# Convolution and routed expert network in one kernel: where a step's copies, the weights' stores and the first rows stand in the order

## Chip, cores and metric

The kernel runs on 1 core of one Trainium2 chip. The metric is the device time of one execution in microseconds (us). Three runs of the kernel before took 964.08, 965.21 and 965.73; the median is 965.21.

## What is computed

```python
def _attn_ref(x, weight_gen):
    w = np.exp(weight_gen - np.max(weight_gen, axis=-1, keepdims=True))
    w = w / (np.sum(w, axis=-1, keepdims=True) + 1e-09)
...
    out = np.einsum('bshk,bskhg->bshg', w, x_unf)

def _moe_ref(x, w_skip, w_gate, w1, w2):
    do_compute = x @ w_skip > 0
    out = x.copy()
    xc = x[do_compute]
    logits = xc @ w_gate
    e_idx = np.argmax(logits, axis=1)
...
    for e in range(E):
        mask = e_idx == e
        h = np.maximum(xc[mask] @ w1[e], 0.0)
        y[mask] = gate_w[mask, None] * (h @ w2[e])
    out[do_compute] = xc + y
```

A causal convolution over 7 positions, with weights that are a softmax per token and head, runs over 8 sequences of 3584 tokens with 192 features. Its output rows go into a mixture of 8 experts with 1024 hidden features: a row with a positive skip score is sent to the expert of its highest gate logit, and the expert's answer, times the gate's softmax, is added to the row. The other rows pass unchanged.

## The kernel before, in words

**Convolution.** The tokens are cut into 16 chunks of 4 steps, 64 steps in all. What a step issues, and in which order, stands in a string of tokens in `SEQ`, one of four by the step's place in its chunk; the engines execute what they are given in that order. The tokens that matter here: `x` loads the step's input (L276); `a`, `b` build band matrices on DVE (L323); `C`, `G` are the convolution's matmuls (L342), `c`, `e` copy their result to SBUF on ACT (L349). `K` (`back`) transposes that result on TensorE (L358) and forms the logits (L361), into three PSUM tiles. `O` (`back_out`) copies these out on ACT: acc twice (L372) and ls (L374). `L`, `l`, `H`, `R`, `r`, `W` turn a chunk's logits into each row's expert and place in the expert's bucket in DRAM, and queue the chunk's 16 scatters. `P` takes one piece of the preparation of the experts' weights. `F` takes one piece of the expert network's flow, sends one scatter on POOL (L483) and advances the clock `tick` by one. `M` assigns a pair (256 rows of one expert), `D` (`ahead`) fetches assigned pairs.

**Weights.** For each expert in turn (`prep_expert`, L201) two raw halves are loaded (L198), ACT takes absolute values with a running sum (L207) whose output goes into the expert's own weight tile, small matmuls and DVE find scales (L213 to L227), POOL clears the tile's last columns (L228), and ACT and DVE split the weights into f16 high and low parts (L229, L235 to L243). Six DMAs on SP store the tile to `wsp` in DRAM (L246 to L249). These tiles have the tag `wst` with 4 buffers, and a pair's fetch takes its tile from the same 4. A fetch (L611) reads the pair's rows from the buckets (L619) and its weights from `wsp` in three DMAs (L631) at a place that a register gives.

**Expert network.** `flow` (L746) takes pairs in turn. `prep_rows` (L634) gives a row scale: absolute sums on ACT (L641), DVE (L644 to L647), the high part on ACT (L650), the low part on DVE (L653, L656), then eight transposes on TensorE (L663), copied by ACT (L664). A pair has four up steps: ten matmuls (L676), the ReLU's f16 high part hh on ACT (L680), the low part hl on DVE (L686), and two steps later twelve down matmuls (L696). The result is added to the rows (L702) and scattered to the output (L707). There are 57 pairs. The first flow starts `LEAD` ticks after its fetch. PSUM has 3 buffers with tag `s` (the three of `K`, the transposes, and others), 3 for the ups and the convolution, 2 for the downs. After the last step only pairs are left, from about 776 us on; this is called the tail.

An F token that falls between K and O is taken only in part:

```python
    def advance(held=False):
        if held and (turning[0] or not ffn[0]):
            return
```

Of the kernel before, what the change touches and what calls it, by code (L numbers as in the profile page):

```python
# [11 lines left out]
F16 = mybir.dt.float16  # L12
F32 = mybir.dt.float32
I32 = mybir.dt.int32
AF = mybir.ActivationFunctionType
# [36 lines left out]
SEQ = [  # L52
# [4 lines left out]
]  # L57
# [4 lines left out]
XG = 6  # L62
LEAD = 5
BEHIND = 2
DEAL = 5
# [10 lines left out]
def conv_moe_kernel(ctx, tc, x, wg, w_skip, w_gate, w, out):  # L76
# [29 lines left out]
    def pop():  # L106
        if outs:
            outs.pop(0)()
        elif unsent:
            send(*unsent.pop(0))  # L110
    wsp = dram.tile([E, P, WC], F16, name="wsp")
    img = [dram.tile([K, P, R_], F32, name=f"img{i}") for i in range(2)]
# [60 lines left out]
    for t in img:  # L173
        nc.sync.dma_start(t.rearrange("m p r -> (m p r)").rearrange("(p c) -> p c", p=P), zero[:, 0:K * R_])

    dummy = cst.tile([P, RW], F32, name="dummy")
    nc.vector.memset(dummy, 0.0)
# [9 lines left out]
    heads = cst.tile([1, 2, E], F32, name="heads")  # L187
    nc.vector.tensor_copy(heads[:, 0, :], iof[:, 0:E])
    nc.vector.tensor_scalar(heads[:, 1, :], ecap[0:1, :], -float(TRASH), None, op0=ALU.add)
# [3 lines left out]
    most = cst.tile([1, E + 1], F32, name="most")  # L193
    nc.vector.memset(most[:, E:E + 1], E * TT * float(P) - 0.5)

    def load_part(e, i):
# [4 lines left out]
    def prep_expert(e, raws):  # L201

        a, b, c = raws[0][:, 0:FF], raws[0][:, FF:], raws[1]
        m = st.tile([P, 2], F32, tag="wm", name="wm")
        wo = sl.tile([P, WC], F16, tag="wst", name="wst", bufs=4)
        for i in range(2):
            nc.scalar.activation(wo[:, 0:3 * FF // 2], raws[i], AF.Abs, accum_out=m[:, i:i + 1])  # L207
            yield
# [10 lines left out]
        nc.tensor.matmul(pm[:, 2 * P:2 * P + 2], ones2, dg, start=True, stop=True)  # L219
        yield  # L220
        mv = st.tile([P, 2], F32, tag="wmv", name="wmv")
        nc.vector.tensor_scalar(mv, pm[:, 2 * P:2 * P + 2], 1e-30, None, op0=ALU.max)
# [20 lines left out]
        nc.vector.scalar_tensor_tensor(wo2[:, :, D:2 * D], c3, s2, wo2[:, :, 0:D], op0=ALU.mult, op1=ALU.subtract)  # L243
        yield
        for i in range(2):
            nc.sync.dma_start(wsp[e, 0:64, 2 * FF + i * FF // 2:2 * FF + (i + 1) * FF // 2], bh[64 * i:64 * (i + 1), :])  # L246
            nc.sync.dma_start(wsp[e, 64:P, 2 * FF + i * FF // 2:2 * FF + (i + 1) * FF // 2], bl[64 * i:64 * (i + 1), :])
        nc.sync.dma_start(wsp[e, :, 0:2 * FF], wo[:, 0:2 * FF])
        nc.sync.dma_start(wsp[e, :, 3 * FF:], wo[:, 3 * FF:])  # L249

# [267 lines left out]
    def assign(T, F, final):  # L518
# [42 lines left out]
        yield  # L561
        nc.vector.tensor_scalar(so[:, :, 0], ef, float(E - 1), None, op0=ALU.min)
        yield
# [5 lines left out]
        yield  # L569
        todo.extend((so, i, T, None) for i in range(F))  # L570
        told.extend([tick[0] + BEHIND] * F)

    def assign_one(T):
# [25 lines left out]
        yield  # L599
        todo.append((so, 0, T, counted[0]))  # L600
        told.append(tick[0] + BEHIND)

# [7 lines left out]

    def fetch(so, i, T, upto):  # L611

        NT = P * T
        er = nc.values_load(so[0:1, i, 0:1], engines=[ET.SP], min_val=0, max_val=E - 1,
                            skip_runtime_bounds_check_because="clamped to the experts on the chip")
# [14 lines left out]
        for c0, c1 in ((0, 2 * FF), (2 * FF, 4 * FF), (4 * FF, WC)):  # L630
            nc.sync.dma_start(wt[:, c0:c1], wsp[ds(er, 1), :, c0:c1].rearrange("a p c -> p (a c)"))  # L631
        return T, wt, xg
# [50 lines left out]
    def up_low(ph, hh):  # L683

        hl = sl.tile([P, 512], F16, tag="hl", name="hl", bufs=3)
        nc.vector.scalar_tensor_tensor(hl, ph, 0.0, hh, op0=ALU.max, op1=ALU.subtract)  # L686
        return hh, hl
# [46 lines left out]
    def pairs():  # L734

        while True:
            if auto[0]:
                ahead(3)
            if not ready:
                return  # L740
            if ready[0][3] + LEAD > tick[0] and not auto[0]:
                return
            T, wt, xg, _ = ready.pop(0)
            yield wt, xg, 0

    def flow():  # L746
# [25 lines left out]
        while cur:  # L772
            py = ps_y.tile([P, 2, 256], F32, tag="py", name="py")
            new = None
            for f2 in range(NFB // 2):
# [8 lines left out]
                while len(done_) > (f2 < 1):  # L784
                    finish(*done_.pop(0))
                late.append((cur, py, f2, up_low(*h)))
                if f2 == 0 and len(rows) < 2:
                    new = begin()
                    if new:
                        rows.append(new)  # L790
                        next(new[1])
                if new and f2 == 1:
                    next(new[1])
                if rows and f2 == 2:
# [11 lines left out]
    def advance(held=False):  # L806
        if held and (turning[0] or not ffn[0]):
            return
        if ffn[0] is None and ready and ready[0][3] + LEAD <= tick[0] and START <= step[0]:
            ffn[0] = flow()  # L810
        elif ffn[0] and next(ffn[0], ffn) is ffn:
            ffn[0] = None
# [196 lines left out]
```

## Time and profile before

| | us |
|---|---|
| median of 3 runs | 965.21 |
| lowest and highest | 964.08, 965.73 |
| profiled execution | 956.43 |
| its span in the profile | 954.5 |
| TensorE busy (PE) | 814.2 (85%) |
| VectorE (DVE) | 659.5 (69%) |
| ScalarE (ACT) | 474.3 (50%) |
| GpSimd (POOL) | 403.9 (42%) |

The span is the profiled stretch of one execution. TensorE's granted clock is 0.927 of full speed on the mean. Busy shares are averages over three very different parts: preparation and convolution to some 160 us, all three kinds of work to 250 us, convolution and experts to 771 us, and the tail. Waits are listed by the engine that waits and the work that ended the wait; SPq is SP's DMA queue, and times are from the span's start.

### The profile page before, as it was taken

Reading aid. Unit: us, or ns where it says so; the run is one execution under the profiler, and the core shown is the slowest. Engines: PE = TensorE matmul, PEld = TensorE weight load, DVE = VectorE, ACT = ScalarE, POOL = GpSimd, SP = SyncE. Lnnn points to the kernel's source line nnn. Section 1 sums busy time; section 2 is a strip of 40 time slices with the busy share of each in tenths; the row PEclk is TensorE's granted clock in tenths of the full one; section 3 lists DMA queues with packets and bytes.
Section 4 is the critical chain, followed back from the end, with each engine's and each line's share of the span. In section 5 each row is a group of like instructions: output and inputs, shape, how many; then the busy total and the mean of one; then the engine's idle time right before and its main releaser. Section 6 shows DMA issues by size and latency. Waiting matters only on the chain. (4 is left out here: it accounts for less than half of the span.)

```text
span 954.5 us, 36775 instructions
## 1 busy us (share of the span) xinstructions
PE 814.2 (85%) x15248; PEld 694.1 (73%) x15248; DVE 659.5 (69%) x1945; ACT 474.3 (50%) x1141; POOL 403.9 (42%) x415
## 2 busy tenths in 40 slices
PE   0567853778799997999899998999999899999997
PEld 0446633567587886888788786887888789899996
DVE  4888974746877785878686876687675566855553
ACT  0456655454555544555445463555555455455552
POOL 1008883243344536354626372545454353712122
PEclk9787775877799997999999999999999999999999
DMA  6588698897687569576868595768576559876540
GB/s 225 179 291 280 223 305 300 303 323 237 193 283 269 187 229 307 169 246 229 261 190 274 174 299 166 245 201 263 189 267 201 164 196 287 272 257 219 194 158 19
DMA packets 99176, 221.33 MB, mean 232 GB/s; under 512 B 16144, under 2 KB 54859, under 8 KB 97216
## 3 DMA queue, kind: packets, MB, share of 16 engines
q1 hardware_dynamic: 81248, 197.22, 62.2%
q0 software_dynamic: 17760, 21.75, 7.2%
q8 instruction: 120, 1.97, 0.8%
q14 instruction: 48, 0.39, 0.1%
HBM read 152.97 MB, written 77.80 MB: 242 GB/s over the span
## 5 line engine op out<-in xcount | busy, mean ns | idle before, releaser
L483 POOL DMA_INDIRECT bucket<-acc,ixi x256 | 279.2, 1091 | 320.9 <-DVE wst L229 68.0
L676 PE MATMUL ph<-xT,wst 128*128 128x256 f16 x2280 | 296.7, 279 | 20.2 <-DVE hl L686 12.8
L676 PEld LDWEIGHTS <-wst 128*128 128x128 f16 x2280 | 219.8, 100 | 59.5 <-issue 22.4
L680 ACT ACTIVATE hh<-ph 128x512 f16<-128x512 f32 x228 | 135.8, 595 | 243.3 <-PE ph L676 239.9
L686 DVE SCALAR_TENSOR_TENSOR hl<-ph,hh 128x512 f16<-128x512 f32 x228 | 155.8, 684 | 144.6 <-ACT hh L680 144.4
L696 PE MATMUL py<-wst,hh 128*128 128x192 f16 x1824 | 247.0, 248 | 0.0
L696 PE MATMUL py<-wst,hl 128*128 128x192 f16 x912 | 225.6, 247 | 2.8 <-issue 1.9
L707 POOL DMA_INDIRECT out_dram<-xg x114 | 117.1, 1027 | 225.5 <-DVE xg L702 171.7
L342 PE MATMUL bt<-bd,xt 64*32 64x56 f32 x8192 | 125.7, 232 | 59.3 <-DVE bd L323 27.9
L696 PEld LDWEIGHTS <-hh 128*128 128x128 f16 x1824 | 164.3, 99 | 15.8 <-issue 9.4
L342 PEld LDWEIGHTS bt<-bd,xt 64*32 64x32 f32 x8192 | 100.9, 113 | 92.2 <-issue 47.3
L323 DVE TENSOR_TENSOR bd<-rot,mask 128x896 f32<-128x896 f32 x128 | 137.0, 1080 | 8.8 <-DMA rot<-img 8.8
L696 PEld LDWEIGHTS <-hl 128*128 128x128 f16 x912 | 89.8, 98 | 3.4 <-issue 2.1
L664 ACT COPY xT<-pt 128x512 f16<-128x512 f16 x114 | 61.4, 590 | 57.2 <-PE pt L663 57.2
L702 DVE SCALAR_TENSOR_TENSOR xg<-py,fc,xg 128x192 f32<-128x192 f32 x114 | 42.2, 411 | 64.7 <-PE py L696 60.6
L349 ACT COPY xs<-bt 128x448 f32<-128x448 f32 x128 | 66.0, 539 | 37.0 <-PE bt L342 36.8
L358 PE MATMUL pa<-ident,xs 128*112 128x128 f32 x512 | 77.8, 298 | 1.6 <-ACT xT L664 1.1
L650 ACT ACTIVATE xs<-xg,rs 128x192 f16<-128x192 f32 x114 | 45.7, 449 | 44.1 <-DVE rs L647 31.0
L358 PEld LDWEIGHTS pa<-ident,xs 128*112 128x112 f32 x512 | 63.1, 147 | 5.1 <-ACT xT L664 2.8
L663 PE MATMUL pt<-ident,xs 128*128 128x128 f16 x456 | 41.7, 226 | 24.0 <-ACT acc L372 13.2
L372 ACT COPY acc<-pa 112x384 f32<-112x384 f32 x128 | 55.0, 481 | 1.6 <-PE pa L358 1.5
L663 PEld LDWEIGHTS <-xs 128*128 128x128 f16 x456 | 30.1, 100 | 31.1 <-DVE xs L656 19.7
(152 smaller groups left out, 734.3 us busy)
## 6 DMA issues: line engine op xcount, KB each, us to landing
wst<-wsp SPq DMA_DIRECT2D x114, 512.0 KB
wst<-wsp SPq DMA_DIRECT2D x57, 520.0 KB
xt<-in_x_dram SPq DMA_DIRECT2D x64, 384.0 KB
out_dram<-acc SPq DMA_DIRECT2D x16, 1358.0 KB
raw<-in_moe_w_dram SPq DMA_DIRECT2D x16, 768.0 KB
xg<-bucket SPq DMA_DIRECT2D x57, 194.0 KB
rot<-img SPq DMA_DIRECT2D x16, 448.0 KB
wt<-in_weight_gen_dram SPq DMA_DIRECT2D x16, 392.0 KB
```

The costliest lines, as they stand in the source:

```text
L323: nc.vector.tensor_tensor(bd.rearrange("p h (m u) -> p h m u", m=K), rot_[c][:, :, i0 * H:(i0 + 2) * H].rearrange("p m h -> p h m").unsque ...
L342: mm = nc.tensor.matmul(bt[a][GP * j:GP * (j + 1), c0:c0 + QH], xt[p0:p1, b0:b0 + GP], bd_[k, i // 2][p0:p1, i % 2 * H + h, :], start=True ...
L349: nc.scalar.copy(xs_[k][:, 2 * a:2 * a + 2, :], bt_[k][a][:, 0:2 * QB * QH].rearrange("p (x c) -> p x c", x=2))
L358: nc.tensor.transpose(pa[j][0:Q, x * P:(x + 1) * P], xs[:, x, j * Q:(j + 1) * Q], ident)
L483: i = nc.gpsimd.indirect_dma_start(out=bviews[t], out_offset=bass.IndirectOffsetOnAxis(ap=rt_[c][:, t:t + 1], axis=0), in_=acc_[c][:, t, : ...
L663: nc.tensor.transpose(pt[:, 2 * i2 + i, :], xs[:, t, i2, i * P:(i + 1) * P], ident16)
L664: nc.scalar.copy(xT[:, :, t * P:(t + 1) * P], pt)
L676: mm = nc.tensor.matmul(ph[:, fi * 2 * P:(fi + 1) * 2 * P], wt[:, a * FF + f0:a * FF + f0 + P], xT[:, cc, :], start=j == 0, stop=j == 4)
L680: nc.scalar.activation(hh, ph, AF.Relu)
L686: nc.vector.scalar_tensor_tensor(hl, ph, 0.0, hh, op0=ALU.max, op1=ALU.subtract)
L696: mm = nc.tensor.matmul(py[:, t, 0:D], l[:, a], w2v[:, f, r, :], start=f == 0 and t == 0 and j == 0, stop=f == NFB - 1 and j == 2, skip_gr ...
L707: i = nc.gpsimd.indirect_dma_start(out=oviews[nsc[0] % 8], out_offset=bass.IndirectOffsetOnAxis(ap=xg[:, t0 + t, D + 1:D + 2].bitcast(I32) ...
```

## The change

Five things change. (1) `wsp` becomes a two-dimensional tensor, and each expert's stores go through a view of its own; a fetch is given by hand the stores of the experts prepared when its pair was assigned. Expert numbers that lead to a fetch are scaled by 128, and one small store writes 30 columns of `wsp` at the start. (2) The absolute values go to a fixed scratch `spare`, and the expert's weight tile is taken five pieces later, after the scale matmuls. (3) `O` stands right behind `K` in each step. (4) In up step 1 the low parts of the next pair's rows (L653, L656) are issued ahead of hl (L686). (5) The first pair is told 4 ticks after its assignment instead of 2, and its flow starts 7 ticks after its fetch instead of 5.

```diff
@@ -50,18 +50,17 @@
 SEQ = [
-    "O x F C a D F G w P L F l D c b T M P F e 2 P F H P F D P T M K F P",
-    "O x F C R a D F G W r R P F W r R D c b T M P F W r e 3 P F P F W D P T M K F P",
-    "O x F C W r R a D P F G W r V P F W D 5 c b T M P F e P F P F D P T M K F P",
-    "O x F C a D P F G 4 P F D c b T M P F e 0 P F P F D 1 P T M K F P",
+    "x F C a D F G w P L F l D c b T M P F e 2 P F H P F D P T M K O F P",
+    "x F C R a D F G W r R P F W r R D c b T M P F W r e 3 P F P F W D P T M K O F P",
+    "x F C W r R a D P F G W r V P F W D 5 c b T M P F e P F P F D P T M K O F P",
+    "x F C a D P F G 4 P F D c b T M P F e 0 P F P F D 1 P T M K O F P",
 ]
...
-LEAD = 5
-BEHIND = 2
+LEAD, BEHIND = (5, 7), (2, 4)
@@ -108,7 +107,9 @@
-    wsp = dram.tile([E, P, WC], F16, name="wsp")
+    wsp = dram.tile([E * P, WC], F16, name="wsp")
+    wviews = dram_disjoint_views(wsp[:, :], E)
+    stored = []
@@ -173,6 +174,7 @@
+    nc.sync.dma_start(wsp[0:1, 6 * FF + 2:WC], zero[0:1, 0:15].bitcast(F16))
@@ -185,7 +187,7 @@
-    nc.vector.tensor_copy(heads[:, 0, :], iof[:, 0:E])
+    nc.vector.tensor_scalar(heads[:, 0, :], iof[:, 0:E], float(P), None, op0=ALU.mult)
@@ -193,6 +195,8 @@
+    spare = cst.tile([P, 3 * FF // 2], F16, name="spare")
@@ -202,9 +206,8 @@
-        wo = sl.tile([P, WC], F16, tag="wst", name="wst", bufs=4)
         for i in range(2):
-            nc.scalar.activation(wo[:, 0:3 * FF // 2], raws[i], AF.Abs, accum_out=m[:, i:i + 1])
+            nc.scalar.activation(spare, raws[i], AF.Abs, accum_out=m[:, i:i + 1])
@@ -218,6 +221,7 @@
         nc.tensor.matmul(pm[:, 2 * P:2 * P + 2], ones2, dg, start=True, stop=True)
         yield
+        wo = sl.tile([P, WC], F16, tag="wst", name="wst", bufs=4)
@@ -242,11 +246,14 @@
+        to = wviews[e][e * P:(e + 1) * P, :]
+        stored.append([])
         for i in range(2):
-            nc.sync.dma_start(wsp[e, 0:64, 2 * FF + i * FF // 2:2 * FF + (i + 1) * FF // 2], bh[64 * i:64 * (i + 1), :])
...
+            stored[e].append(nc.sync.dma_start(to[0:64, half], bh[64 * i:64 * (i + 1), :]).ins)
...
+        stored[e].append(nc.sync.dma_start(to[:, 0:2 * FF], wo[:, 0:2 * FF]).ins)
+        stored[e].append(nc.sync.dma_start(to[:, 3 * FF:], wo[:, 3 * FF:]).ins)
@@ -597,8 +604,8 @@
-        todo.append((so, 0, T, counted[0]))
-        told.append(tick[0] + BEHIND)
+        todo.append((so, 0, T, counted[0], n))
+        told.append(tick[0] + BEHIND[given[0] == 1])
@@ -628,7 +635,10 @@
         for c0, c1 in ((0, 2 * FF), (2 * FF, 4 * FF), (4 * FF, WC)):
-            nc.sync.dma_start(wt[:, c0:c1], wsp[ds(er, 1), :, c0:c1].rearrange("a p c -> p (a c)"))
+            i = nc.sync.dma_start(wt[:, c0:c1], wsp[ds(er, P), c0:c1])
+            if paced[0]:
+                for j in chain(*stored[:most_e]):
+                    after(i, j, "the weights of an expert")
@@ -783,14 +793,14 @@
+                if new and f2 == 1:
+                    next(new[1])
                 late.append((cur, py, f2, up_low(*h)))
                 if f2 == 0 and len(rows) < 2:
                     new = begin()
                     if new:
                         rows.append(new)
                         next(new[1])
-                if new and f2 == 1:
-                    next(new[1])
@@ -806,7 +816,7 @@
-        if ffn[0] is None and ready and ready[0][3] + LEAD <= tick[0] and START <= step[0]:
+        if ffn[0] is None and ready and ready[0][3] + LEAD[spent[0] == 0] <= tick[0] and START <= step[0]:
```

**ACT, around the first pair's rows.** xs,S are its sums (L641, L651 in the change), raw the weights of e5. Before:

```order
L641 ACTIVATE xs,S_2525<-xg 128x192 x2
L389 COPY L<-lt 112x4x2x9 x2
L349 COPY xs_2536<-bt 128x448
L650 ACTIVATE xs<-xg,rs 128x192 x2
L349 COPY xs_2536<-bt 128x448
L207 ACTIVATE wst,wm<-raw 128x1536 x2
L372 COPY acc<-pa 112x2x192 x2
L374 COPY ls<-pl 128x224
L664 COPY xT<-pt 128x4x128 x2
L427 ACTIVATE dl<-dl 112x128
L680 ACTIVATE hh<-ph 128x512
```

With the change:

```order
L356 COPY xs_2530<-bt 128x448 x2
L210 ACTIVATE spare,wm<-raw 128x1536 x2
L379 COPY acc<-pa 112x2x192 x2
L381 COPY ls<-pl 128x224
L651 ACTIVATE xs,S_2606<-xg 128x192 x2
L434 ACTIVATE dl<-dl 112x128
L660 ACTIVATE xs<-xg,rs 128x192 x2
L449 COPY qf<-rk 128x136
L356 COPY xs_2722<-bt 128x448 x2
L674 COPY xT<-pt 128x4x128 x2
L239 ACTIVATE wst<-raw,wsc 128x1024
L690 ACTIVATE hh<-ph 128x512
```

The sums stood at the head of this piece, in front of the L copies; now the L copies stand above the piece and the sums behind the absolute values and the step's acc and ls copies. The first split of e5 (L239) now stands ahead of the first hh.

**SP and DVE, the stores of e4 and the first write into e5's tile**, with the semaphores waited for (DMAHW lanes are used by SP's DMAs in turn). SP before, then with the change:

```order
L246 DMA wsp<-wst 64x512 [waits DMAHW3_49,DMAHW4_49,DMAHW1_49,DMAHW7_49,DMAHW0_49,Activation_49]
L247 DMA wsp<-wst 64x512 [waits DVE_49]
L246 DMA wsp<-wst 64x512 [waits DMAHW5_49]
L247 DMA wsp<-wst 64x512 [waits DMAHW6_49]
L248 DMA wsp<-wst 128x2048
L249 DMA wsp<-wst 128x3104 [waits DVE_49,Activation_49,Pool_49]
```

```order
L253 DMA wsp<-wst 64x512 [waits DMAHW2_49,DMAHW4_49,DMAHW1_49,DMAHW5_49,DMAHW0_49,Activation_49]
L254 DMA wsp<-wst 64x512 [waits DVE_49]
L253 DMA wsp<-wst 64x512 [waits DMAHW6_49]
L254 DMA wsp<-wst 64x512 [waits DMAHW7_49]
L255 DMA wsp<-wst 128x2048
L256 DMA wsp<-wst 128x3104 [waits DVE_49,Pool_49]
```

DVE before, then with the change, around the write of e5's scale into its tile (L229, L233):

```order
L227 TENSOR_TENSOR wsc<-wsc,wsf 128x2 [waits DVE_49]
L229 TENSOR_SCALAR wst<-wmv 128x1 [waits DMAHW3_49,DMAHW2_49,DMAHW7_49,DMAHW0_49,Pool_49]
L580 SCALAR_TENSOR_TENSOR most<-most,pick 1x8
L584 TENSOR_REDUCE bm<-most 1x1 [waits DVE_49]
L587 TENSOR_SCALAR bo<-most,bm 1x8 [waits DVE_49]
L590 TENSOR_TENSOR bb<-heads,bo 1x16 [waits DVE_49]
L592 SCALAR_TENSOR_TENSOR heads<-bo,heads 1x8 [waits DVE_49]
L238 SCALAR_TENSOR_TENSOR wst<-raw,wsc,wst 128x1024 [waits DMAHW5_49,Activation_49]
```

```order
L231 TENSOR_TENSOR wsc<-wsc,wsf 128x2 [waits DVE_49]
L233 TENSOR_SCALAR wst<-wmv 128x1 [waits DMAHW5_49,DMAHW4_49,DMAHW6_49,DMAHW1_49,DMAHW7_49,DMAHW0_49,Pool_49]
L587 SCALAR_TENSOR_TENSOR most<-most,pick 1x8
L591 TENSOR_REDUCE bm<-most 1x1 [waits DVE_49]
L594 TENSOR_SCALAR bo<-most,bm 1x8 [waits DVE_49]
L597 TENSOR_TENSOR bb<-heads,bo 1x16 [waits DVE_49]
L599 SCALAR_TENSOR_TENSOR heads<-bo,heads 1x8 [waits DVE_49]
L242 SCALAR_TENSOR_TENSOR wst<-raw,wsc,wst 128x1024 [waits Activation_49]
L696 SCALAR_TENSOR_TENSOR hl<-ph,hh 128x512 [waits Activation_49]
```

The first store waits for five lanes in both, moved by one. DVE's write waited for four lanes and POOL and now waits for six lanes and POOL; hl stands behind it. The six lanes 4, 5, 6, 7, 0, 1 are those that e4's six stores have in turn.

**DVE, up step 1 of a pair in the tail** (S is the next pair's row sums). Before:

```order
L644 TENSOR_SCALAR S_17973<-S_17973 128x2
L645 TENSOR_SCALAR S_17973<-S_17973 128x2
L647 RECIPROCAL rs<-S_17973 128x2
L702 SCALAR_TENSOR_TENSOR xg<-py,fc,xg 128x192 x2
L686 SCALAR_TENSOR_TENSOR hl<-ph,hh 128x512
L653 SCALAR_TENSOR_TENSOR xs<-xg,rs,xs 128x192 x2
L656 COPY xs<-xs 128x2x64 x2
L686 SCALAR_TENSOR_TENSOR hl<-ph,hh 128x512
L666 SCALAR_TENSOR_TENSOR fc<-S_17973,wst,xg 128x2
```

With the change:

```order
L654 TENSOR_SCALAR S_17975<-S_17975 128x2
L655 TENSOR_SCALAR S_17975<-S_17975 128x2
L657 RECIPROCAL rs<-S_17975 128x2
L712 SCALAR_TENSOR_TENSOR xg<-py,fc,xg 128x192 x2
L663 SCALAR_TENSOR_TENSOR xs<-xg,rs,xs 128x192 x2
L666 COPY xs<-xs 128x2x64 x2
L696 SCALAR_TENSOR_TENSOR hl<-ph,hh 128x512 x2
L676 SCALAR_TENSOR_TENSOR fc<-S_17975,wst,xg 128x2
```

L653 and L656 moved ahead of the hl that stood in front of them.

## Rows read from the trace of the kernel before

**Rows 1.** Windows view: stretch, length; busy of PE, PEld, DVE, ACT, POOL; clock, DMA share, GB/s.
```profile
140.00:160.00 20.00, 10.20 (x173) 7.64 (x173) 8.13 (x21) 8.00 (x18) 9.79 (x13) 0.50 0.83 275
...
180.00:200.00 20.00, 14.38 (x235) 11.40 (x233) 9.34 (x20) 10.68 (x20) 8.14 (x8) 0.86 0.97 349
776.00:940.00 164.00, 159.41 (x1721) 147.43 (x1720) 99.43 (x335) 85.61 (x213) 52.45 (x55) 1.00 0.65 216
```

**Rows 2.** ACT's timeline from 157 to 203 us (start, duration, instruction, idle before and releaser).
```profile
157.05 0.36 ACT L641 ACTIVATE xs<-xg 128x192 f16<-128x192 f32 x1 [9.65 <-DMA xg<-bucket]
...
163.49 0.36 ACT L374 COPY ls<-pl 128x224 f32<-128x224 f32 x1
...
170.87 0.60 ACT L680 ACTIVATE hh<-ph 128x512 f16<-128x512 f32 x1 [3.57 <-PE ph L676]
...
179.53 1.15 ACT L235 ACTIVATE wst<-raw,wsc 128x1024 f16<-128x1024 f32 x1 [4.80 <-DVE wsc L227]
...
181.67 1.56 ACT L240 ACTIVATE wst<-raw,wsc 128x1536 f16<-128x1536 f32 x1
...
183.87 0.36 ACT L374 COPY ls<-pl 128x224 f32<-128x224 f32 x1
...
195.69 1.48 ACT L207 ACTIVATE wst<-raw 128x1536 f16<-128x1536 f32 x1 [6.26 <-PE py L696]
...
202.94 0.36 ACT L374 COPY ls<-pl 128x224 f32<-128x224 f32 x1
```

**Rows 3.** SP's timeline, the issues of weights and their stores, 154 to 180 us.
```profile
154.45 0.41 SPq L619 DMA_DIRECT2D xg<-bucket  x1
...
170.21 0.51 SPq L246 DMA_DIRECT2D wsp<-wst  x1
...
173.36 0.37 SPq L249 DMA_DIRECT2D wsp<-wst  x1
...
179.38 2.21 SPq L631 DMA_DIRECT2D wst<-wsp  x3
```

**Rows 4.** SP's waits over the program (total us, times, longest).
```profile
SPq L246 <- DMA wst<-wsp: 28.2, 6, 8.2
```

**Rows 5.** ACT's timeline in the tail, the hh at equal places of two pairs.
```profile
809.63 0.60 ACT L680 ACTIVATE hh<-ph 128x512 f16<-128x512 f32 x1 [1.49 <-PE ph L676]
...
818.87 0.60 ACT L680 ACTIVATE hh<-ph 128x512 f16<-128x512 f32 x1 [1.49 <-PE ph L676]
```

**Rows 6.** TensorE's waits over the whole program.
```profile
PE pt L663 <- ACT acc L372: 13.2, 4, 4.2
```

**Rows 7.** TensorE's waits from 300 to 771 us.
```profile
PE ph L676 <- DVE hl L686: 8.0, 12, 1.6
PE pt L663 <- ACT acc L372: 6.1, 2, 3.6
```

**Rows 8.** DVE's timeline at one pair of the tail.
```profile
813.48 0.68 DVE L686 SCALAR_TENSOR_TENSOR hl<-ph,hh 128x512 f16<-128x512 f32 x1
814.08 0.74 DVE L653 SCALAR_TENSOR_TENSOR xs<-xg,rs,xs 128x192 f16<-128x192 f32 x2
814.85 0.29 DVE L656 COPY xs<-xs 128x128 f16<-128x128 f16 x2
```

**Rows 9.** TensorE's timeline: the rows' transposes and next up, with and without a wait.
```profile
814.58 0.22 PE L663 MATMUL pt<-ident,xs 128*128 128x128 f16 x1
...
815.50 1.26 PE L676 MATMUL ph<-xT,wst 128*128 128x256 f16 x10
...
258.06 0.61 PE L663 MATMUL pt<-ident,xs 128*128 128x128 f16 x8
258.51 1.25 PE L676 MATMUL ph<-xT,wst 128*128 128x256 f16 x10
```

**Rows 10.** TensorE's waits in the tail, 776 to 940 us.
```profile
PE pt L663 <- DVE xs L656: 3.3, 17, 0.3
```

**Rows 11.** TensorE's timeline, the program's first up.
```profile
168.89 1.94 PE L676 MATMUL ph<-xT,wst 128*128 128x256 f16 x10
```

More of the change, by code (lines that the diff above doesn't have):

```diff
@@ L244, in prep_expert @@
         yield
+        to = wviews[e][e * P:(e + 1) * P, :]
+        stored.append([])
         for i in range(2):
-            nc.sync.dma_start(wsp[e, 0:64, 2 * FF + i * FF // 2:2 * FF + (i + 1) * FF // 2], bh[64 * i:64 * (i + 1), :])
-            nc.sync.dma_start(wsp[e, 64:P, 2 * FF + i * FF // 2:2 * FF + (i + 1) * FF // 2], bl[64 * i:64 * (i + 1), :])
-        nc.sync.dma_start(wsp[e, :, 0:2 * FF], wo[:, 0:2 * FF])
-        nc.sync.dma_start(wsp[e, :, 3 * FF:], wo[:, 3 * FF:])
+            half = slice(2 * FF + i * FF // 2, 2 * FF + (i + 1) * FF // 2)
+            stored[e].append(nc.sync.dma_start(to[0:64, half], bh[64 * i:64 * (i + 1), :]).ins)
+            stored[e].append(nc.sync.dma_start(to[64:P, half], bl[64 * i:64 * (i + 1), :]).ins)
+        stored[e].append(nc.sync.dma_start(to[:, 0:2 * FF], wo[:, 0:2 * FF]).ins)
+        stored[e].append(nc.sync.dma_start(to[:, 3 * FF:], wo[:, 3 * FF:]).ins)
     prepared, open_, prepares = [0], [0], [0]
@@ L561, in assign @@
         yield
-        nc.vector.tensor_scalar(so[:, :, 0], ef, float(E - 1), None, op0=ALU.min)
+        nc.vector.tensor_scalar(so[:, :, 0], ef, float(E - 1), float(P), op0=ALU.min, op1=ALU.mult)
         yield
@@ L569, in assign @@
         yield
-        todo.extend((so, i, T, None) for i in range(F))
-        told.extend([tick[0] + BEHIND] * F)
+        todo.extend((so, i, T, None, E) for i in range(F))
+        told.extend([tick[0] + BEHIND[0]] * F)
     def assign_one(T):
@@ L609, in together, with fetch @@
                     gs.remove(g)
-    def fetch(so, i, T, upto):
+    def fetch(so, i, T, upto, most_e):
         NT = P * T
-        er = nc.values_load(so[0:1, i, 0:1], engines=[ET.SP], min_val=0, max_val=E - 1,
+        er = nc.values_load(so[0:1, i, 0:1], engines=[ET.SP], min_val=0, max_val=(E - 1) * P,
                             skip_runtime_bounds_check_because="clamped to the experts on the chip")
@@ L740, in pairs @@
                 return
-            if ready[0][3] + LEAD > tick[0] and not auto[0]:
+            if ready[0][3] + LEAD[0] > tick[0] and not auto[0]:
                 return
```

## The prediction

> **What bounds the kernel now.** I read the stretches first [rows 1]. From 776 us on only the expert network (FFN) is left: TensorE is busy 159.41 of 164 us, at full clock. So little can be won per pair there, but what is won counts in full, since nothing else sets the end. Between 140 and 200 us the picture is the opposite: TensorE is busy 10.2 of the first 20 us and 14.4 of the last 20, the granted clock is 0.50 and 0.86 there, and the DMA share 0.83 and 0.97. That is the stage in which the convolution runs, the experts' weights are still prepared, and the first pairs start.
>
> What stops that stage is seen on ACT [rows 2], whose copies of the logits (ls, L374) mark the end of each step. Step 16 ends at 163.49, step 17 at 183.87 and step 18 at 202.94, so the last two take 20.4 and 19.1 us. Two stalls stand inside. **Stall A**: ACT waits 9.65 us, until 157.05, for the rows of the first pair; everything in ACT's queue waits with it. **Stall B**: ACT waits 6.26 us, until 195.69, to write absolute values of e6's weights into a weight tile whose last user is pair 0's final down matmul. Between them ACT starts e5's split at 179.53 after 4.80 us.
>
> SP shows why the rows come late and what follows [rows 3]: the fetch of pair 0 goes out at 154.45, and after pair 1's SP stands until 170.21 in front of e4's weight stores. That wait is for the pairs' own weight loads [rows 4], 28.2 us in 6 times, 8.2 the longest. The last of e4's stores is issued at 173.36; pair 2's weights, which must not be read before these stores, go at 179.38 and SP shows no wait for them, so they have landed by then.
>
> **The change, part by part.**
>
> *Views of the weights in DRAM, the extra small store, scaled heads.* The order shows that the first store of e4 still waits for five DMA lanes, the same set as before moved by one, because one DMA more was issued ahead. I therefore count on the wait of [rows 4] staying: 0 us. If the views did remove it, e4's stores could leave 8.2 us earlier, at 162; that is a rival below. The extra store is one DMA issue on SP, about 0.4 us by the 0.41 of [rows 3], in the opening stage where SP is ahead: 0, at most 0.4.
>
> *Absolute values to a scratch, first rows later.* These two act on the same stage and are counted together. The order on ACT shows the first pair's L641 behind the step's Abs and its acc and ls copies instead of ahead of the L copies. What was queued behind the 9.65 us is no longer behind it, so step 16 can end some 8 us sooner. But the weight tile of e5 is now taken five pieces later, after pairs 0, 1 and 2 have taken theirs, so it falls to the tile that e4 was stored from. ACT's first split of e5, DVE's scale (L229 before) and POOL's memset must then wait for all six of e4's stores. Those leave only at 170.21 to 173.36, for a reason that the change does not touch. They land after 173.36+0.37 and by 179.38; I take 178, near the later end, because the DMA stays loaded and raw weights are queued behind. Behind that wait stand on ACT the first hh, step 17's copies, and on DVE the first hl and the next band; TensorE and the scatters follow them.
>
> So step 17 is not freed. From the start of e5's split, ACT needed 183.87-179.53=4.34 us to reach ls. In the new order the third split (1.56 us at 181.67) comes behind the copies, leaving about 2.8 to 3.3: 178+3.2=181.2, a gain of about 2.7 us at step 17. In exchange the first hh, at 170.87 before, is behind the same wait, and by the order 1 instead of 3 up groups have been issued at that point. Stall B then goes entirely, since Abs needs no weight tile: 6.3 us, of which I count 5, since e6's own first write now waits for e5's stores, which are late next. Together steps 17 and 18 come about 8 us earlier, with 2 up groups owed. A full up step (10 ups and 12 downs) costs a quarter of a pair; the hh of 809.63 and 818.87 are four apart, so 9.24/4=2.3 us [rows 5], and the debt is 4.6 us, repaid in a stage where TensorE is the bound. Net 8-4.6=3.4. The transposes that waited for the acc copies in this stage (L663 behind L372: 13.2 us in 4 over the whole program, of which 6.1 in 2 after 300 us [rows 6, 7], so 7.1 in 2 here) give about a third more, 2.6, the rest lying inside stalls already counted. **Early stage: -6.** Bounds: all of A, B and the 4.80 gone without a debt would be 20.7; I take -16 as the far end since the DMA share is 0.97 from 180 to 200 and bytes do not shrink. The other end is +6: no gain, and 2 up groups plus some clock.
>
> *A step's copies right behind its transposes.* After 300 us this takes away pt<-acc, 6.1 us in 2 [rows 7]; some of it returns, because hh and the preparation's pieces now stand behind the copies. *Rows' parts ahead of low parts* shows in the steady stage the other way round: hl now follows 1.03 us of L653 and L656, and ph<-hl is already 8.0 us in 12 there [rows 7]. I take **-2** for both, between -6 and +3.
>
> *Rows' parts ahead of low parts, in the tail.* Here the price can be read [rows 8, 9]. On DVE the hl of 813.48 stands ahead of L653 (814.08) and L656 (814.85, two copies to 815.14). TensorE starts the first transpose at 814.58 and the next up at 815.50, 0.92 later, with a wait for L656 in between. Where nothing waited, at 258.06, the next up (258.51) follows 0.45 after the first transpose. With hl behind, the rows' parts end about 0.6 earlier, at 814.5, in time. So at most 0.47 us a pair is won; the wait is shown 17 times, 17x0.47=8.0 in all. The idle alone is 3.3 us in those 17 [rows 10], the lower end. I take 0.36 a pair, nearer the upper end, because the idle counts empty time alone, while the distance from start to start is what the next up sees: 17x0.36=6, **-6**, from -3 to -8. What covers the hl that now ends near 815.2: its down matmuls come behind the whole next up (1.26 us from 815.50), so not before 816.7. If that cover were gone, the 0.6 would come back on TensorE.
>
> **Sum.** -6-2-6=-14. The profiled execution took 956.43 us (its span is 954.5 and 1.9 lie around it); 956.43-14=942.4. The median of the runs shown is 965.21, 8.8 above the profiled one, so the forecast is **951 us**.
>
> **The clock, read against a rule.** At 168.89 the ten matmuls of an up took 1.94 us, at 815.50 1.26 [rows 9, 11]; the granted clock of 0.50 from 140 to 160 is the lower of its two levels (1.2 of 2.4 GHz), and it is 0.86 from 180 to 200 [rows 1]. The first ups now come about 8 us later. If the clock then stayed at the lower level through 180 to 200, the 14.38 us of TensorE work there would be 14.38x0.86/0.50=24.7, which is 10.3 more: 951+10=961. The Trainium skill ("TensorE: Matmul & The Clock Gate", section "Part 1: The HAM clock gate") says that the throttled state is the default and that activity releases it; by that rule a later start of the FFN speaks for this case. The rows agree in direction. But the convolution's matmuls go on in that stretch and will be denser, so I give it 0.06.
>
> **Rivals.**
> 1. *The stall only moves* (0.20). e5's split waits for e4's stores past 179 and the 2 owed groups eat the rest: early gain 0, the other -8 stay: 965.2-8=957. For it: the unchanged store wait [rows 4]. Against it: stall B is gone in any case.
> 2. *The views free the stores* (0.12). They leave by 162, e5 never waits, and A, B and the 4.80 go nearly in full, less the debt: 20.7-4.6=16 and 8 more: 965.2-24=941. Against it: the lane list in the order.
> 3. *The low parts take the tail's gain back* (0.08): early -6, the rest 0: about 959.
> 4. *Slower* (0.09). The wait on e4's stores is the place. Step 17's end was at 183.87, 3.2 us behind that wait ending; once the stores land after about 181, the step ends later than before. Then POOL's scatters stand behind the memset too, the next fetches wait for scatters, and each lost step costs a full FFN step of 2.3 us. It outweighs the 8 us of tail and steady stage from a landing of about 185 on: 185+3.2-183.9=4.3, with 4.6 of debt and nothing left of stall B's gain, less 8, makes 966; at 190 it is 971.
>
> **How the numbers follow.** The forecast has 0.45, the clock 0.06. About 0.2% (1.9 us) is what a measurement of this kernel can tell from no change, so "same" is 963.3 to 967.1. The forecast and rivals 1 to 3 are faster at their centres (0.85), the clock case mostly so; of their upper ends and of rival 4's lower end I put 0.09 into same. Faster 0.82, same 0.09, slower 0.09. The range goes from rival 2's 941 to 962: above it lie rival 4 and the upper ends, below it only the lower half of rival 2.
>
> **What would show it.** Right: ACT shows no wait of several us at the first rows, nor one at Abs; instead ACT or DVE waits for wsp<-wst at e5, until 176 to 180; SP still waits for wst<-wsp at the stores; ls of step 18 falls near 195; in the tail pt<-xs is gone from TensorE's waits and four hh take 8.7 to 8.8 us. Wrong: SP's store wait gone (rival 2), a wait for wsp<-wst beyond 185 (rival 4), py or ph waiting for hl in the tail (rival 3), a clock of 0.5 after 185.

## The result, and the profile after

The changed kernel took 970.05 us (median of 22 runs, 961.11 to 977.52), the kernel before 961.31 (22 runs). The ratio is 1.0074, with a 95% interval of 1.0045 to 1.0103: slower by 0.7%, where 951 us and a gain were forecast. The ratio is that of the runs within 1.5% of their kernel's fastest, 20 of each 22, and so not that of these medians. The profiled execution of the changed kernel took 967.01 us with a span of 965.3, against 956.43 and 954.5.

The marks at which a step's last copy (ls) starts, with the up groups issued by then, cut the span into the prediction's stages:

| stage | before, us (ups) | after, us (ups) | difference | for equal ups (2.3 us each) |
|---|---|---|---|---|
| start to step 18 | 202.94 (6) | 195.21 (4) | -7.7 | -3.1 |
| start to step 23 | 277.18 (20) | 264.21 (18) | -13.0 | -8.4 |
| step 23 to step 63 | 494.0 (133) | 525.1 (136) | +31.1 | +24.2 |
| step 63 to the end of the span | 183.3 (75) | 176.0 (74) | -7.3 | -5.0 |

The last three differences add to +10.8, the difference of the spans. The early stage and the tail won about what was forecast, and the middle lost 24 us where 2 were to be won. In that middle the mark of step 31 is still 1.3 us ahead (370.33 against 371.67); step 40 is 0.4 behind, step 47 5.0, step 63 18.1.

**Early stage** [rows 2, 3, 4]. ACT's timeline of the changed kernel (start, duration, instruction, idle before and what ended it):

```profile
156.06 0.36 ACT L651 ACTIVATE xs<-xg 128x192 f16<-128x192 f32 x1 [3.21 <-DMA xg<-bucket]
...
176.40 1.15 ACT L239 ACTIVATE wst<-raw,wsc 128x1024 f16<-128x1024 f32 x1 [13.23 <-DMA wsp<-wst]
...
179.27 0.36 ACT L381 COPY ls<-pl 128x224 f32<-128x224 f32 x1
...
195.21 0.41 ACT L381 COPY ls<-pl 128x224 f32<-128x224 f32 x1
```

The rows are waited for 3.21 us instead of 9.65, and e5's split waits 13.23 us for e4's stores, until 176.40. No Abs waits for a weight tile. SP's timeline and, below it, SP's waits over the program:

```profile
153.54 0.42 SPq L626 DMA_DIRECT2D xg<-bucket  x1
...
167.96 0.51 SPq L253 DMA_DIRECT2D wsp<-wst  x1
...
171.11 0.39 SPq L256 DMA_DIRECT2D wsp<-wst  x1
```

```profile
SPq L253 <- DMA wst<-wsp: 27.4, 5, 8.1
```

The stores still stand behind the pairs' weight loads, 27.4 us in 5 where it was 28.2 in 6.

**Tail** [rows 8, 9, 10]. TensorE's waits from 794 to 952 us, then its timeline at one pair (the transposes, and the ups around them):

```profile
PE pt L673 <- DVE xs L666: 0.4, 1, 0.4
```

```profile
873.15 1.25 PE L686 MATMUL ph<-xT,wst 128*128 128x256 f16 x10
...
875.23 0.61 PE L673 MATMUL pt<-ident,xs 128*128 128x128 f16 x8
875.67 1.26 PE L686 MATMUL ph<-xT,wst 128*128 128x256 f16 x10
...
877.76 1.25 PE L686 MATMUL ph<-xT,wst 128*128 128x256 f16 x10
```

From the up before the transposes to the up after them it is 2.52 us, to the one behind that 2.09, so four make 3x2.09+2.52=8.79, as forecast (8.7 to 8.8).

**The middle** [rows 7]. The windows view of the changed kernel (stretch, length; busy of PE, PEld, DVE, ACT, POOL; clock, DMA share, GB/s), then of the kernel before:

```profile
160.00:180.00 20.00, 8.23 (x86) 6.07 (x88) 7.12 (x27) 4.68 (x11) 2.15 (x4) 0.59 0.85 303
180.00:200.00 20.00, 15.34 (x308) 12.62 (x292) 12.15 (x32) 12.03 (x27) 7.52 (x8) 0.71 0.97 353
264.20:789.30 525.10, 475.93 (x9212) 406.87 (x9212) 361.08 (x1103) 257.05 (x654) 237.76 (x235) 0.97 0.67 217
789.30:965.30 176.00, 167.53 (x1837) 158.00 (x1834) 104.93 (x347) 87.61 (x218) 59.20 (x62) 0.99 0.62 205
```

```profile
277.20:771.20 494.00, 463.46 (x9092) 396.03 (x9093) 357.62 (x1096) 248.80 (x647) 234.12 (x233) 0.98 0.70 229
771.20:954.50 183.30, 172.26 (x1858) 159.55 (x1855) 105.19 (x347) 89.06 (x221) 59.51 (x63) 0.99 0.59 197
```

TensorE was idle 525.1-475.93=49.2 us between steps 23 and 63, against 494.0-463.46=30.5. Its waits in that stretch, of the changed kernel and then of the kernel before:

```profile
PE ph L686 <- DVE hl L696: 15.2, 13, 1.9
PE bt L349 <- issue: 11.2, 7, 4.6
PE bt L349 <- DVE hl L696: 7.6, 8, 1.2
PE lt L388 <- issue: 2.9, 1, 2.9
PE lt L388 <- ACT acc L379: 2.5, 1, 2.5
```

```profile
PE ph L676 <- DVE hl L686: 8.2, 13, 1.6
PE pt L663 <- ACT acc L372: 6.1, 2, 3.6
PE bt L342 <- issue: 5.2, 3, 3.4
PE bt L342 <- DVE hl L686: 2.1, 7, 0.6
```

Waits for hl went from 8.2+2.1=10.3 [rows 7 show 8.0 of these from 300 us on] to 22.8. One place shows how. DVE, ACT and TensorE of the changed kernel at 489 us:

```profile
489.29 0.38 DVE L427 TENSOR_REDUCE rc<-oh 112x8 f16<-112x128 f16 x1
489.58 0.74 DVE L712 SCALAR_TENSOR_TENSOR xg<-py,fc,xg 128x192 f32<-128x192 f32 x2
490.23 0.74 DVE L663 SCALAR_TENSOR_TENSOR xs<-xg,rs,xs 128x192 f16<-128x192 f32 x2
491.01 0.29 DVE L666 COPY xs<-xs 128x128 f16<-128x128 f16 x2
491.22 0.68 DVE L696 SCALAR_TENSOR_TENSOR hl<-ph,hh 128x512 f16<-128x512 f32 x1
```

```profile
488.08 0.57 ACT L690 ACTIVATE hh<-ph 128x512 f16<-128x512 f32 x1
```

```profile
491.96 2.30 PE L686 MATMUL ph<-xT,wst 128*128 128x256 f16 x10 [1.91 <-DVE hl L696]
...
496.37 0.61 PE L673 MATMUL pt<-ident,xs 128*128 128x128 f16 x8
```

hh was ready at 488.65. DVE was still in the chain that picks experts (L427 ends 489.67), then did the rows' result (xg), then the next pair's low parts (L663, L666: 1.03 us), and only then hl, at 491.22. TensorE stood 1.91 us, because the up needs the PSUM tile that hl reads. The transposes that want the low parts came at 496.37, five us after these were ready: here the new order bought nothing. By DVE's timeline the hl stood directly behind these parts in 13 of the 21 waits for hl; these 13 make 18.9 of the 22.8 us, and without the parts' own time in front they would be 12.8 us shorter (an estimate from this timeline).

The up behind the wait took 2.30 us; where nothing waited it takes 1.26 [rows 9]. That is the clock and not the wait as such: eleven of the 13 ups that waited for hl took 1.25 to 1.27 us. Here the granted clock fell to the lower of its two levels at the end of the wait. It did so too within 1.2 us of the end of the two other waits of 1.91 us, those of the ups at 282.61 and 600.72 (windows view, columns as above):

```profile
284.00:287.00 3.00, 3.00 (x78) 2.61 (x68) 2.45 (x9) 0.68 (x2) 1.15 (x2) 0.50 0.64 201
492.10:495.00 2.90, 2.90 (x73) 1.99 (x72) 0.88 (x2) 0.71 (x2) 0.46 (x1) 0.50 0.66 260
601.30:604.50 3.20, 3.20 (x77) 2.35 (x75) 1.62 (x4) 0.76 (x2) 1.17 (x2) 0.50 0.56 218
```

Between the marks of steps 23 and 63 the lower level was granted for 34 us in all, and in the kernel before for 20.

### The profile page after: what moved, and what is told of

Its sections match the earlier page's. It is cut to its first block, busy times and chain, and to the rows that moved or that the text cites. A ratio compares the mean times of both kernels' runs of the same rounds, so it can differ in the third digit from the quotient of the medians.

```text
span 965.3 us, 36806 instructions
## 1 busy us (share of the span) xinstructions
PE 809.2 (84%) x15248; PEld 693.4 (72%) x15248; DVE 661.2 (68%) x1945; ACT 478.0 (50%) x1141; POOL 408.8 (42%) x415
## 5 line engine op out<-in xcount | busy, mean ns | idle before, releaser
L686 PE MATMUL ph<-xT,wst 128*128 128x256 f16 x2280 | 295.7, 278 | 27.2 <-DVE hl L696 19.9
L686 PEld LDWEIGHTS <-wst 128*128 128x128 f16 x2280 | 219.2, 100 | 66.3 <-issue 24.3
L349 PE MATMUL bt<-bd,xt 64*32 64x56 f32 x8192 | 130.0, 235 | 79.5 <-DVE bd L330 27.6
L349 PEld LDWEIGHTS bt<-bd,xt 64*32 64x32 f32 x8192 | 103.1, 114 | 114.7 <-issue 55.9
L673 PE MATMUL pt<-ident,xs 128*128 128x128 f16 x456 | 37.3, 226 | 9.7 <-DVE xs L666 4.9
L368 PE MATMUL pl<-xs,gt 128*32 128x224 f32 x512 | 41.2, 397 | 4.4 <-DVE wmv L226 4.4
```

The costliest lines, as they stand in the source:

```text
L349: mm = nc.tensor.matmul(bt[a][GP * j:GP * (j + 1), c0:c0 + QH], xt[p0:p1, b0:b0 + GP], bd_[k, i // 2][p0:p1, i % 2 * H + h, :], start=True ...
L686: mm = nc.tensor.matmul(ph[:, fi * 2 * P:(fi + 1) * 2 * P], wt[:, a * FF + f0:a * FF + f0 + P], xT[:, cc, :], start=j == 0, stop=j == 4)
```

## The experiments

Three theories were set against each other. R: rows' parts ahead of hl make hl late in the steps. O: the copies right behind the transposes hold ACT back. P (phase, from the ninth run on): it matters at which places of a step the pairs' up steps fall, which start and copies both set.

The runs e1 to e4 went to one chip, e5 to e8, e9 to e12 and e13 to e16 each to another. On these four chips the kernel before takes 1112 to 1123 us (medians), 16% more than in the first runs; each kernel is compared with the kernel before on its own chip. "hl waits" are TensorE's waits for hl (ups and convolution together) from step 23 to 63 in that kernel's profile, "acc waits" those of the transposes for acc.

| run | start | copies | rows' parts | views, scratch | ratio to before (95%) | hl waits | acc waits |
|---|---|---|---|---|---|---|---|
| e9 (before) | old | old | after hl | no, no | 1 | 6.4 | 7.8 |
| e8 | old | old | first in tail | no, no | 0.9976 (0.9942 to 1.0011) | 5.6 | 0.8 |
| e2 | old | old | first | no, no | 1.0041 (1.0007 to 1.0075) | 11.5 | 3.4 |
| e4 | old | new | after hl | no, no | 1.0049 (1.0019 to 1.0080) | 6.1 | 11.5 |
| e12 | late | old | after hl | no, no | 0.9981 (0.9948 to 1.0014) | 6.8 | 3.1 |
| e15 | late | new | first in tail | no, no | 0.9837 (0.9794 to 0.9881) | 12.8 | 0 |
| e5, the change | late | new | first | yes, yes | 0.9935 (0.9902 to 0.9969) | 23.3 | 0 |
| e13, the change | late | new | first | yes, yes | 0.9871 (0.9817 to 0.9925) | 24.7 | 0 |
| e1 | late | new | first in tail | yes, yes | 0.9769 (0.9722 to 0.9816) | 11.8 | 0 |
| e6, as e1 | late | new | first in tail | yes, yes | 0.9772 (0.9728 to 0.9815) | 12.1 | 0 |
| e14, as e1 | late | new | first in tail | yes, yes | 0.9775 (0.9725 to 0.9826) | 13.6 | 0 |
| e3 | late | old | first | yes, yes | 0.9885 (0.9831 to 0.9938) | 12.6 | 0.8 |
| e7 | late | old | first in tail | yes, yes | 0.9871 (0.9820 to 0.9921) | 6.8 | 4.7 |
| e10 | old | new | first | yes, yes | 1.0115 (1.0057 to 1.0174) | 14.8 | 10.5 |
| e11 | late | new | first | yes, no | 0.9873 (0.9805 to 0.9941) | 22.7 | 0 |
| e16 | late | new | first in tail | yes, no | 0.9812 (0.9763 to 0.9861) | 12.8 | 0 |

**Rows' parts and low parts: e1, e6, e14 against e5, e13; e2, e8.** Edit of e1, e6 and e14, to the changed kernel (e8 makes the same order in the kernel before; e2 takes the change's order into it):

```diff
-                if new and f2 == 1:
+                if new and f2 == 1 and auto[0]:
                     next(new[1])
                 late.append((cur, py, f2, up_low(*h)))
...
+                if new and f2 == 1 and not auto[0]:
+                    next(new[1])
```

> The changed kernel, but with the rows' parts (L663, L666) ahead of hl only after the last convolution step; in the steps hl comes first again. Theory R (the parts ahead of hl make hl late, so the ups and the convolution wait for the PSUM tiles that hl frees): against the changed kernel, ph<-hl and bt<-hl fall from 15.2 and 7.6 us between 264 and 789 us to about 8 and 2, and the time falls by 12 or more, to 0.99 to 0.998 of the kernel before. Theory O (the copies right behind the transposes hold ACT back): no change against the changed kernel, about 1.007 of before.

> The same kernel as the first experiment, beside the changed kernel this time. Theory R: faster than the changed kernel by 8 us or more, with the hl waits of TensorE between steps 23 and 63 at most half of the changed kernel's. Theory O: the same as the changed kernel, within 3 us.

> The changed kernel itself, as the control for the other kernels on this chip (another chip than that of the first pair of traces ran the kernel before in 1114 us instead of 961). Theory R: where the convolution's steps are long, hl has slack and the early gain of 13 us stays, 0.985 to 0.998 of before; where they run as in the first traces, about 1.007. Theory O: about 1.007 on either.

> The changed kernel as the control of this call. On a chip like those before: 0.99 to 0.997 of before, hl waits of TensorE from step 23 to 63 of 22 to 24 us. On a chip like that of the first pair of traces (before at about 961): 1.004 to 1.01.

> The changed kernel with the rows' parts ahead of hl in the tail alone. Theory R: 12 to 20 us faster than e13 whatever the chip, with hl waits of about 12 us in the steps. If the loss in the first pair came from elsewhere (the copies or the start), the gain there would be under 5 us.

> The kernel before with the rows' parts ahead of hl everywhere and nothing else changed. Theory R: the tail wins 5 to 6 us, the steps lose 10 to 15 (hl waits of TensorE from 10 to over 20 us from step 23 on), 1.004 to 1.01 of before. Theory O: only the tail's gain shows, 0.993 to 0.996 of before.

> The kernel before with the rows' parts ahead of hl in the tail alone: the price of that term by itself. Both theories: TensorE's wait pt<-xs goes in the tail and the time falls by 5 to 7 us, 0.993 to 0.995 of before.

Measured: with hl first in the steps the change is faster by 0.9935-0.9772=1.63% on one chip (18 us) and by 0.96% on another (11 us, just under the 12 to 20 that R gave; there the intervals of the two ratios still touch). TensorE's waits from step 23 to 63, e5 and then e6:

```profile
PE ph L686 <- DVE hl L696: 11.8, 8, 1.9
PE bt L349 <- DVE hl L696: 11.5, 8, 2.4
```

```profile
PE bt L349 <- DVE hl L696: 6.6, 7, 1.3
PE ph L686 <- DVE hl L696: 5.5, 7, 0.9
```

and on the other chip e13, then e14:

```profile
PE ph L686 <- DVE hl L696: 13.8, 8, 1.9
PE bt L349 <- DVE hl L696: 10.9, 8, 2.4
```

```profile
PE bt L349 <- DVE hl L696: 6.6, 7, 1.3
...
PE ph L686 <- DVE hl L696: 7.0, 10, 0.9
```

The waits fall to about half, as theory R expects: 11.2 and 11.1 us less. Between steps 23 and 63 the profiles show 603.8 (e5) and 590.8 us (e6) for the same ups, 610.6 (e13) and 601.7 us (e14). The windows view of this stage, e5 and then e6:

```profile
303.55:907.31 603.76, 523.45 (x9232) 433.75 (x9231) 361.88 (x1105) 256.98 (x654) 239.65 (x235) 0.92 0.57 187
301.95:892.76 590.81, 510.35 (x9226) 422.24 (x9227) 360.66 (x1105) 255.54 (x654) 234.40 (x235) 0.95 0.59 191
```

TensorE's idle time is 80.3 us in e5 and 80.5 in e6: it did not fall with the waits for hl, since others grew. What fell is the busy time for the same work, by 13.1 us, at a granted clock of 0.95 instead of 0.92; from e13 to e14 it is 7.6 us of busy time and 1.3 of idle time, at 0.94 instead of 0.92. Over the whole program the clock of e5's twelve runs is 0.867 to 0.888, that of e6's six 0.886 to 0.902. In this stage e5 has nine waits for hl of over 1.5 us and e13 ten, e6 and e14 have none. So the order costs 11 to 18 us on these chips, and the profiles show this time as clock more than as idle time. That the long waits bring the clock down fits the falls in the first trace, but no run separates the two.

With the old copies the same order costs less: e2 against e8, in the kernel before, is 0.65%, and e3 against e7, in the change, 0.14%, each on different chips. In e2 and e3 only 6 and 7 waits for hl have it directly behind the rows' parts, in e5 and e13 11 and 12. e2 landed at the low end of what R gave and outside what O gave. The bounds against the kernel before that R gave for e1 (0.99 to 0.998) were too high, since the change itself is ahead on these chips. e8 alone is not separated from no change: 2.7 us by its centre, where 5 to 7 were expected, so the tail's term is smaller on these chips or hidden in their spread. e5 came out on R's side of 1. e13 came out below its bounds (0.99 to 0.997), with 24.7 us of hl waits where 22 to 24 were given.

**Copies and start: e3, e7, e4, e10, e12.** e3 and e7 put the old strings into the change and into e1's version; e4 takes the new strings into the kernel before. e10 and e12:

```diff
-LEAD, BEHIND = (5, 7), (2, 4)
+LEAD, BEHIND = (5, 5), (2, 2)
```
(e10, in the change; e12 makes the late start in the kernel before.)

> The changed kernel with the four step strings of the kernel before, so that a step's copies (O) open the next step again. Theory O: the loss of about 24 us between steps 23 and 63 goes, 0.985 to 0.99 of before. Theory R: the loss stays, and the waits of the transposes for acc come back, some 3 to 6 us, 1.005 to 1.015 of before.

> The changed kernel with both parts undone in the steps: the old step strings, and the rows' parts ahead of hl in the tail only. Theory O: the fastest of the four, by 10 us or more against the one that undoes the rows' order alone. Theory R: within 5 us of that one, 0.975 to 0.99 of before.

> The kernel before with the copies right behind the transposes and nothing else changed. Theory O: slower by 10 to 20 us, 1.01 to 1.02 of before. Theory R: the 13.2 us of transposes waiting for acc go, of which 3 to 6 us are kept, 0.994 to 0.998 of before.

> The changed kernel with the first pair told after 2 ticks and started 5 ticks after its fetch, as before; 156 ups are issued by step 63 instead of 154, as in the kernel before with the new copies. Theory P: the stretch from step 23 to 63 goes back to 615 to 620 us, the time to 1.003 to 1.01 of before. Theory R: the stretch stays at 604 plus the price of its ups; the early stage loses the 8 to 13 us that the later start earned, about 1.0 of before.

> The kernel before with the later telling and start alone; by the order 155 ups are issued by step 63 instead of 153. Theory P: the stretch from step 23 to 63 changes by more than 8 us either way beside the price of the ups. Theory R: it does not; the early stage gains 8 us at step 18 less a debt of 2 ups, 0.994 to 0.998 of before.

> The kernel before, for its profile on such a chip. If the hl waits decide (theory R), its ph<-hl and bt<-hl between steps 23 and 63 add to under 12 us where the changed kernel's came to 23; the stretch between these steps takes 604 to 608 us for 133 ups, as in the kernel before with the tail's term alone. If it is the place at which the pairs' up steps meet the steps (theory P, phase), the sum of hl waits is no guide, and the waits for acc and for xs differ as much.

Measured: the copies have no price of their own. With the old start they lose (e4 +0.5%, and e10 is the slowest of all); with the late start and hl first they win 1.0% (e6 against e7, one chip); with the late start and the rows' parts first (e5 and e13 against e3, on different chips) no sign is settled. TensorE's waits in e10, then in the kernel before (e9):

```profile
PE pt L673 <- ACT acc L379: 10.5, 6, 2.7
PE bt L349 <- DVE hl L696: 8.0, 6, 1.8
PE ph L686 <- DVE hl L696: 6.8, 8, 1.8
```

```profile
PE bt L342 <- issue: 54.3, 127, 1.3
PE pt L663 <- ACT acc L372: 7.8, 4, 4.2
PE ph L676 <- DVE hl L686: 4.0, 7, 1.0
...
PE bt L342 <- DVE hl L686: 2.4, 6, 0.8
```

With the old start and new copies the transposes of the rows stand behind the step's own transposes and wait for acc, 10.5 us here and 11.5 in e4; in the change, in e1, e6 and e14 there is none. Theory O falls: e7 was not the fastest, e4's loss is half of the least that O gave, and e3, which is in O's bounds against the kernel before, is so only because the change is ahead there already. R's bounds fail too: for e7 (within 5 us of e6) it was 11 us, for e4 a gain was given, for e3 a loss, for e10 about 1.0, and the stage from step 23 to 63 in e9 took 597.1 us where 604 to 608 were given (e8, with the same order in its steps on another chip, took 606.5, so single profiles of this stage compare only roughly across chips). e12 is at the edge of R's bounds and not separated from 1. Theory P, that start and copies act through where an up step meets a step, is borne out for the acc waits by e4, e10, e6 and e12; for the total it gave e10's sign and roughly its size (1.003 to 1.01 expected, 1.0115 measured; 618.6 us for the middle, 615 to 620 expected), but for e12 a change of the middle of over 8 us, where 602.5 us with 137 ups against 597.1 with 133 is 3.8 us less after four ups' 9.2.

**Scratch and views: e11, e15, e16.** e11 and e16 take the weight tile before Abs again, in the change and in e1's version; e15 has the new copies, late start and tail order in the kernel before, with its stores.

```diff
+        wo = sl.tile([P, WC], F16, tag="wst", name="wst", bufs=4)
         for i in range(2):
-            nc.scalar.activation(spare, raws[i], AF.Abs, accum_out=m[:, i:i + 1])
+            nc.scalar.activation(wo[:, 0:3 * FF // 2], raws[i], AF.Abs, accum_out=m[:, i:i + 1])
...
-        wo = sl.tile([P, WC], F16, tag="wst", name="wst", bufs=4)
```

> The changed kernel with the absolute values in the expert's weight tile, taken at the start as before. The order of the ups by step stays. Prediction's step on stall B: ACT waits again 5 to 7 us at Abs of e6 for a pair's last down, and the wait of e5's split for e4's stores goes; net 0 to 6 us slower than the changed kernel, 0.994 to 1.0 of before. Rival: the stall has slack, no change, 0.993.

> The kernel before with the new copies, the late start and the rows' parts first in the tail, but with its own weight stores and with absolute values in the weight tile. If views and scratch bring nothing: the same as e14 within 4 us. Prediction's step on stalls: the 6 to 7 us wait at Abs of e6 comes back, 5 us slower than e14.

> As e14 with the absolute values in the weight tile again, views kept. If the scratch brings nothing: the same as e14 within 4 us. Prediction's step on stall B: 5 us slower than e14.

Measured: the wait at Abs comes back, as forecast in size, for a store instead of a down (ACT's waits from 186 to 310 us in e11):

```profile
ACT wst L211 <- DMA wsp<-wst: 6.8, 1, 6.8
```

In e15 and e16 it is 6.5 and 6.4 us. Step 23 then ends at 308.65 (e11) instead of 303.55 (e5, on another chip). The total doesn't show it: e11 is not slower than the change was on the other chips (and below both bounds given for it), and e16 and e15 stand 0.4% and 0.6% above e14 with overlapping intervals, so whether the 5 us are kept is not settled. e15's SP waits 25.3 us in 5 for the pairs' loads, e14's 21.5 in 4: the views change nothing that these runs can tell.

## Why the prediction was wrong, point by point

- *Views: 0.* Right: SP's wait stayed, 27.4 us in 5.
- *e5's tile falls to e4's stores.* Right, to 2 us: the split started at 176.40 (178 forecast), step 17 ended at 179.27 (181.2), step 18 at 195.21 (near 195). The first ups were 1 and 4 by then, as the order said. By step 23 the gain was 8.4 us after the debt; 6 was forecast.
- *Tail: -6.* Right: 5.0 us for equal ups, the 17 waits for xs reduced to one of 0.4 us.
- *Steady stage: -2, between -6 and +3.* **This step failed.** It was +24.2. The text saw that "hl now follows 1.03 us of L653 and L656" and that ph<-hl was 8.0 us already, and then set the price of that against 6.1 us of acc waits, with +3 as the end. The acc waits went (6.1 to none). But the other user of the three PSUM tiles, the convolution's bt, was left out (2.1 to 7.6 us), and 1.03 us was taken as something a pair can mostly absorb: 34 pairs pass in this stage, so their far end was 34x1.03=35 us, not +3. DVE is busy 361 of 525 us there and works in order: at 489 us the 1.03 stood behind the chain and the rows' result, and all of it was TensorE's. In the tail no step's chain or band stands in DVE's queue at that point, and TensorE waits 0.2 us for hl in all: there the same edit wins. Experiments on two other chips show the price of this order: undoing it in the steps alone takes away 11 us of hl waits and 11 to 18 us of time. On the chip of the first runs the cause is read from the trace. The forecast also had no term for the clock in this stage, and the clock fell behind each of the three longest waits for hl.
- *Copies: waits for acc go.* Right for the waits in the middle (6.1 us to none); ahead of step 23 one of 4.1 us stayed. That the new place also makes hl later was not seen: with hl first, e6 has 12.1 us of hl waits, e7 with the old copies 6.8; e6 is the faster by 11 us all the same.
- *The slower rival.* Its number (966 to 971) is near the result, its place is not: e4's stores landed by 176.4, well ahead of its 185.
- *The clock case.* From 180 to 200 us the granted clock was 0.71, where it had been 0.86 [rows 1], and 0.59 in the 20 us before that, in most of which the ups stood behind the wait for e4's stores. That is the direction of the Trainium skill's rule ("TensorE: Matmul & The Clock Gate", section "Part 1: The HAM clock gate"), that throttled is the default state. It did not decide: step 18 came as forecast all the same.
- *The base.* The three runs that the forecast started from had a median of 965.21; 22 runs have 961.31. That moves the forecast by 3.9 us and not its sign.

What stays open: the rise of the hl waits explains 12.5 us, half of the 24.2. TensorE was idle 18.7 us more in this middle and, beyond the three ups' 6.9, busy 5.6 us more. Of the idle time, waits with no releaser shown before bt rose by 6.0 us, those of the logits by 5.4, and the acc waits fell by 6.1. The busy time is about what the clock took: 14 us more at half speed are 7 us. No experiment ran on a chip that runs the kernel before in 961 us, so that this remainder belongs to the change, and not to that execution, is not shown. On the other chips the loss of the middle does not come back: for equal ups the change's 603.8 (e5) and 610.6 us (e13) are 0.2 less and 6.6 more than the 597.1 of the kernel before (e9), though its hl waits rise by 17 and 18 us there. Nor is e1's version shown to be faster than the kernel before on such a chip; on three others it is, by 2.2 to 2.3%, and it is the fastest version of the study.

## What to carry to other kernels

An edit that shortens a wait in one stage should be priced in each other stage on the queue that it moves: the same two instructions ahead of hl won 5 us in the tail of the first two profiles, where DVE was free, and cost 11 to 18 us on two chips in the steps, where its queue was full. Multiply the delay by how often it can occur before setting a bound. If the sign differs, make the order depend on the stage, as e1 does in one line. And list every engine queue and buffer that the delayed instruction releases, not only the consumer that one has in mind.

## What the runs showed of the hardware that was not expected

- On the four chips of the experiments the convolution's matmuls wait again and again with no releaser shown: bt<-issue is 54.3 us in 127 in the kernel before (above), 5.2 in 3 in its first profile. On these chips the change is faster than the kernel before, with the same hl waits; a verdict for one chip did not hold for another.
- In the tail of e5's profile DVE stands still for 18.9 us, and TensorE for 11.4 with it (DVE's timeline, then TensorE's). The profile names no releaser on the core; the cause was not settled. It is no single case: e1, e6, e10, e11 and e13 to e16 show DVE idle for 14 to 19 us once in the tail as well, the first two profiles not at all, so the tails on these chips don't measure the tail's term.
- In the first profile of the change the granted clock fell to its lower level behind all three waits of 1.91 us for hl, in the midst of matmul work at the higher level (rows above).

```profile
965.23 0.74 DVE L712 SCALAR_TENSOR_TENSOR xg<-py,fc,xg 128x192 f32<-128x192 f32 x2 [18.91 <-remote]
```

```profile
966.98 0.93 PE L673 MATMUL pt<-ident,xs 128*128 128x128 f16 x7 [11.38 <-DVE xs L666]
```
